# Softmax reciprocals on their way through DRAM: 16 bytes a partition instead of single elements, in an adaLN block on one core

## The chip, the cores and the metric

One Trainium2 chip, one of its cores. A core has five engines that run side by side, each its own list of instructions in order: TensorE (PE) for matmuls, VectorE (DVE), ScalarE (ACT), GpSimd (POOL) and SyncE (SP). Here SP issues nearly all DMA transfers, and 16 DMA engines carry them out. Engines wait for each other, and for transfers, by semaphores. The metric is the device time of one execution in microseconds (us), as the median of several runs.

## The reference

One transformer block, sequence 2048, width 576, in float32. Attention has 32 query heads on 16 cached key/value heads of width 128, and looks at the last 512 cached keys.

```python
h = layernorm(x) * (1 + ca) + sa
q = (h @ wq) per head                       # 32 heads of 128
scores = q @ k[last 512 keys]^T * 128**-0.5
p = softmax(scores); o = p @ v              # two query heads share a k and a v
x = x + ga * (o @ wo)
h = layernorm(x) * (1 + cb) + sb
x = x + gb * ((sigmoid(h @ w_gate) * (h @ w_up)) @ w_down)
```

sa, ca, ga, sb, cb, gb are six rows of silu(c) @ w_mod. The change touches the softmax's division alone: o is the unnormalised product with v, times one over the row's sum.

## The kernel before

The kernel runs in stages: the projection of q (to about 460 us), attention (about 460 to 2380 us), the product with wo, and the gated feed-forward part. All float32 operands are split in a high and a low part, and products are made of three matmuls each.

**Attention** is a list of 128 blocks (`NBLK`). A block is one head and 512 query rows, in four tiles of 128 rows (`TPB` = 4). A loop (lines 1296 to 1325) takes one step n for each tile, so a block is four steps. The step works on several blocks at once, in a software pipeline: `scores` three steps ahead (three matmuls of 128x512 into the tile st, and on VectorE the negated row maximum neg), `expo` two steps ahead (ScalarE writes pp, the exponentials, and their row sum into one column of sum), `transp` (four TensorE transposes of pp into pt; ScalarE and VectorE copy them out, high and low, into ptt), and `pv` five steps behind (three matmuls a step into ot, the output with its 128 features on the partitions and 512 query rows along the free dimension). Tasks that are due at a step's start or end stand in tables (`at_n`, `at_late`).

**The division.** After the fourth tile of block b, VectorE takes the reciprocal of sum (128 partitions x 4 tiles, line 814) into rs. In rs a query row is a partition and a column; in ot a query row is a place in the free dimension, the same for every partition. So rs has to be turned and copied to all partitions, and that goes by way of DRAM: `put_rs` (line 874) stores rs in a scratch tensor rscr of 2 KB, and `get_rs` (line 877) reads it back, broadcast to all 128 partitions, into rb (128x512). Four scratch tensors are used in turn. `ov_out` (line 860) then multiplies ot by rb on VectorE into ov. For the last two blocks the turn is made with TensorE (`spread_rs`, `spread_mm`), and rscr isn't used; so there are 126 stores and 126 reads.

In steps: block b's sums are complete in step 4b+1. `put_rs` is due at the end of step 4b+2, `get_rs` at the end of 4b+5, and `ov_out` at the end of 4b+10.

**SP's list** holds all of this in the order of the program: put_rs, get_rs, a load of q for a later block (qr from qscr), every second block a store of ov (to oscr), every eighth block loads of k and v (kv), and the background work: weights of wo, w_gate, w_up and w_down are loaded into rooms (x, xr), combined and split by GpSimd and ScalarE, and stored in DRAM for the later stages (wosc, dsc, wsc), 5 to 28 transfers a job, a job about every two blocks. The read in get_rs needs the store in put_rs to have landed, so SP stops at get_rs until then, with everything behind it. VectorE in its turn stops at ov_out's multiplication until rb has landed, and behind that stand neg and ptt, which TensorE and ScalarE need.

In the store of before, rscr is laid out tile by tile (4 x 128), and a partition's four values go to four places that are 512 bytes apart, so that each value is a piece of its own, of 4 bytes.

Nearly every instruction is recorded on line 36, a helper, so that the profile is read by the names of the tiles.

Of the kernel before, what the change touches and what calls it, by code (L numbers as in the profile page):

```python
# [9 lines left out]
F32 = mybir.dt.float32  # L10
# [6 lines left out]
P = 128  # L17
BLK = 512
TPB = BLK // P
# [25 lines left out]
def adaln_block_kernel(ctx: ExitStack, tc: tile.TileContext, x, k_cache, v_cache, wq, wo, w_gate, w_up, w_down,  # L45
                       c, w_mod, out):
    early = [True]
    nc = Ordered(tc, early, tc.nc)
# [15 lines left out]
    NBLK = NB * H  # L64
# [5 lines left out]
    dram = ctx.enter_context(tc.tile_pool(name="dram", bufs=1, space=bass.MemoryType.DRAM))  # L70
# [32 lines left out]
    def keep_order(i):  # L103
        if held[0]:
            tc.keep_in_program_order(i)
# [638 lines left out]
    SUM, RS, RB, PP, PT, OT, OP_ = {}, {}, {}, {}, {}, {}, {}  # L744
# [10 lines left out]
    def blk_of(b):  # L755
        return seq[b]
# [46 lines left out]
    def expo(n):  # L803
        b, i = divmod(n, TPB)
        half, hd, blk = blk_of(b)
        if n % 3 == 2 and n < N - 9:
            PP[n] = pools["wp2"].tile([P, W], F32, tag="pp", name="pp", bufs=1)
        else:
            PP[n] = at.tile([P, W], F32, tag="pp", name="pp", bufs=2)
        keep_order(nc.scalar.activation(PP[n], ST.pop(n), AF.Exp, bias=NEG[b][:, i : i + 1],  # L810
                                        accum_out=SUM[b][:, i : i + 1]))
        if i == TPB - 1:
            RS[b] = at.tile([P, TPB], F32, tag="rs", name="rs", bufs=3)
            nc.vector.reciprocal(RS[b], SUM[b])
            if b < NBLK - 2:
                at_late(n - 1, put_rs, b)
                at_late(n + 2, get_rs, b)
            else:
                spread_rs(b)
                at_late(n + (0 if b == NBLK - 2 else 1), spread_mm, b)  # L820
            if last_of[half * H + hd] == b:
                m = n + (5 if b == NBLK - 1 else 9)
                if not summed(half, hd):
                    at_late(m, put_o, half, hd)
                elif hd % 2:
                    at_late(n + 8, sum_o, hd)
                    at_n(n + 15, put_sx, hd, (0, 1))
                    at_n(n + 15, put_o, half, hd - 1)
                    at_n(n + 19, put_o, half, hd)
                    at_late(n + 19, sum_last, hd)  # L830
                    at_n(n + 24, put_sx, hd, (2,))
# [14 lines left out]
    def pv(b, k):  # L846
        half, hd, blk = blk_of(b)
        if k == 0:
            OP_[b] = bank("ot", 2, pools["psa"])
        v = VS[hd // REP]  # L850
        t = PT[b]
        mm_seq(OP_[b], three(v[:, 0, k, :], v[:, 1, k, :], t[:, 0, k, :], t[:, 1, k, :]),
               first=k == 0, last=k == KT - 1)
        if k == KT - 1:
            if b < NBLK - 2:
                at_late(TPB * b + 10, ov_out, b)
            else:
                ov_out(b)

    def ov_out(b):  # L860
        half, hd, blk = blk_of(b)
        unit = (half, hd)
        if unit not in OT:
            own = b // 2 % 4 == 3 and b < NBLK - 12
            OT[unit] = pools["wp2" if own else "ov"].tile([P, TPB, 2, P], F32, tag="ov", name="ov", bufs=1 if own else 3)
        by_tile = RB.pop(b).rearrange("p (i q) -> p i q", i=TPB)
        nc.vector.tensor_mul(OT[unit][:, :, blk % 2, :], OP_[b].rearrange("p (i q) -> p i q", i=TPB), by_tile)
        del OP_[b]

    rscr = [dram.tile([TPB, P], F32, tag=f"rscr{i}", name=f"rscr{i}") for i in range(4)]  # L870
    oscr = [[dram.tile([P, TPB, 4, 4, P], F32, tag=f"oscr{h}_{q}", name=f"oscr{h}_{q}") for q in range(H // 8)]
            for h in range(2)]

    def put_rs(b):
        keep_order(nc.sync.dma_start(rscr[b % 4].rearrange("t p -> p t"), RS[b]))

    def get_rs(b):
        RB[b] = pools["at2"].tile([P, BLK], F32, tag="rb", name="rb", bufs=2)
        keep_order(nc.sync.dma_start(RB[b], rscr[b % 4].rearrange("t p -> (t p)").partition_broadcast(P)))

    def spread_rs(b):
        DG[b] = at.tile([P, TPB, P], F32, tag="qt", name="dg", bufs=2)
# [414 lines left out]
    for n in range(NLO, N + TPB + 5):  # L1297
# [12 lines left out]
        b, i = divmod(n - 5, TPB)  # L1310
# [349 lines left out]
    for v in range(VISITS):  # L1660
        q, pair, t = VISIT[v]
        banks = {}
        for s, (plane, combo, tag, row, col) in enumerate(STAGES):
# [5 lines left out]
            p = banks[tag]  # L1669
# [192 lines left out]
```

## Time and profile before

| | |
|---|---|
| time, median of 3 runs | 3988.19 us (3988.03 to 3992.52) |
| the profiled execution | 3987.48 us, its span from the first to the last instruction 3985.7 us |
| PE / DVE / ACT / POOL busy | 81% / 55% / 46% / 46% of the span |
| granted TensorE clock, mean of the span | 0.90 |
| attention, window 470 to 2340 us | PE busy 1163.82 of 1870 us, granted clock 0.80 |
| DMA over the span | 637.25 MB in 558469 packets, 159 GB/s |

A row of a group in the profile names engine, operation, the tile written and the tiles read, the shape, and how often; behind the bar stand the busy time in us, the mean of one in ns, and the idle time of the engine just before such instructions with what ended it. A row of waits names the engine and what it wrote, what it waited for, the sum in us, how often, and the longest. A row of windows has the stretch, then for PE, its weight loads, DVE, ACT and POOL the busy time with the number of instructions, and last the granted clock, the busy share of the 16 DMA engines and the GB/s that they moved. "SPq" is SP issuing: a DMA's row on SP shows its issue and not its transfer. The chain of waits is followed back from the last instruction; a piece in it that begins with DMA reaches from the transfer's issue to what it released.

### The profile page before, as it was taken

To read this page: it belongs to the slowest core of one execution; us is meant where nothing else is said; L and a number is where in the kernel's file an instruction comes from. 1 tells how busy PE (TensorE), PEld (TensorE's weight loads), DVE (VectorE), ACT (ScalarE), POOL (GpSimd) and SP (SyncE) were. 2 spreads that over 40 slices of the span, in tenths; PEclk is the share of its full clock that TensorE was granted. 3 is DMA by queue.
4 is the path that set the end of the run, shared out by engine and by line. 5 is a ranking of instruction groups with operands and counts; after the bars stand their busy time and mean duration, and the time that the engine had idled before them with its cause. 6 is when DMAs were issued, how large, how long until landed. Compare 5 with 4: busy or idle time off the path is not lost.

```text
span 3985.7 us, 49960 instructions
## 1 busy us (share of the span) xinstructions
PE 3209.4 (81%) x16375; PEld 2696.1 (68%) x16375; DVE 2200.4 (55%) x3908; ACT 1819.5 (46%) x3663; POOL 1845.6 (46%) x1685
## 2 busy tenths in 40 slices
PE   8989865665666666665566669999999999999999
PEld 6767654444554444444445559998888888888888
DVE  6775443343443444333434448887666667666667
ACT  5554443444444444433334334465444445444443
POOL 4646333444555455321221115523676555565555
PEclk9999987787888788777788879999999999999999
DMA  5748787876898677786867964576556555655554
GB/s 171 244 137 240 194 133 131 153 167 134 157 157 169 147 170 148 157 135 128 135 127 93 129 153 179 216 256 205 167 149 171 163 141 160 190 142 144 142 143 120
DMA packets 558469, 637.25 MB, mean 160 GB/s; under 512 B 104576, under 2 KB 478208, under 8 KB 549504
## 3 DMA queue, kind: packets, MB, share of 16 engines
q1 hardware_dynamic: 557072, 633.53, 67.0%
q8 instruction: 129, 2.11, 0.3%
q14 instruction: 132, 1.08, 0.1%
q10 hardware_dynamic: 1136, 0.53, 0.0%
HBM read 426.64 MB, written 207.25 MB: 159 GB/s over the span
## 4 chain that ended last, share of the span: by engine, by line
PE 46%; DMA 37%; SPq 6%; DVE 4%; issue 3%; ACT 2%; POOL 2%; ACTq 0%; POOLq 0%; DVEq 0%
PE a L36 19%; DMA rscr<-rs 19%; PE w L36 10%; PE c L36 10%; SPq L36 6%; DMA rb<-rscr 5%; PE b L36 5%; DMA qr<-qscr 3%; DMA wosc<-xr 1%; DMA dsc<-xr 1%; DMA dsc<-x 1%; DMA oscr<-ov 1%; PE ot L36 1%; DMA qscr<-qo 1%; DMA wsc<-xr 1%
## 5 line engine op out<-in xcount | busy, mean ns | idle before, releaser
L36 PE MATMUL ot<-ptt,vs 128*128 128x512 f32 x1536 | 534.7, 463 | 534.4 <-DVE ptt L36 534.1
L36 PEld LDWEIGHTS ot<-ptt,vs 128*128 128x128 f32 x1536 | 336.2, 226 | 659.4 <-DVE ptt L36 584.5
L36 ACT ACTIVATE pp<-st,neg 128x512 f32<-128x512 f32 x512 | 351.1, 686 | 662.8 <-DVE neg L36 658.6
L36 PE MATMUL a<-hc,sw 128*128 128x512 f32 x2016 | 584.9, 396 | 1.4 <-DVE v L36 1.3
L36 PE MATMUL st<-kt,qt 128*128 128x512 f32 x1536 | 558.3, 477 | 12.8 <-DVE kt L36 12.7
L36 POOL TENSOR_TENSOR qt<-qr,qt 128x512 fp32r<-128x512 f32 x128 | 163.9, 1280 | 837.4 <-ACT qt L36 810.6
L36 DVE TENSOR_TENSOR x<-w,x 128x288 f32<-128x288 f32 x964 | 418.6, 451 | 238.5 <-PE w L36 235.0
L36 DVE TENSOR_TENSOR ptt<-pt,ptt 128x512 fp32r<-128x512 f32 x512 | 352.5, 689 | 271.0 <-ACT ptt L36 270.7
L36 DVE TENSOR_TENSOR ov<-ot,rb 128x512 f32<-128x512 f32 x128 | 88.5, 691 | 742.9 <-DMA rb<-rscr 723.9
L36 PE MATMUL pt<-ident,pp 128*128 128x128 f32 x2048 | 361.3, 306 | 99.0 <-DVE ptt L36 99.0
L36 PEld LDWEIGHTS pt<-ident,pp 128*128 128x128 f32 x2048 | 296.8, 161 | 199.0 <-DVE ptt L36 116.6
L36 PEld LDWEIGHTS a<-hc,sw 128*128 128x128 f32 x2016 | 356.4, 188 | 41.8 <-DVE v L36 2.8
L36 ACT ACTIVATE ptt<-pt 128x512 fp32r<-128x512 f32 x512 | 304.9, 596 | 160.1 <-PE pt L36 159.0
L36 DVE TENSOR_REDUCE neg<-st 128x1 f32<-128x512 f32 x512 | 348.9, 681 | 7.2 <-PE st L36 7.1
L36 ACT ACTIVATE sw<-sr 128x384 fp32r<-128x384 f32 x504 | 257.5, 519 | 190.9 <-issue 90.1
L36 PEld LDWEIGHTS w<-wh,hl 128*128 128x128 f32 x1776 | 297.1, 188 | 52.7 <-DVE x L36 3.1
L36 PE MATMUL w<-wh,hl 128*128 128x288 f32 x1776 | 328.2, 296 | 0.8 <-DVE x L36 0.7
L36 PEld LDWEIGHTS st<-kt,qt 128*128 128x128 f32 x1536 | 296.1, 222 | 45.0 <-DVE kt L36 13.4
L36 POOL TENSOR_TENSOR sw<-sr,sw 128x256 fp32r<-128x256 f32 x245 | 184.7, 754 | 281.9 <-ACT sw L36 279.0
L36 PE MATMUL c<-hc,sw 128*128 128x512 f32 x1008 | 304.0, 395 | 0.0
L36 DVE TENSOR_TENSOR sw<-sr,sw 128x256 fp32r<-128x256 f32 x259 | 188.6, 729 | 141.6 <-ACT sw L36 140.3
L36 POOL TENSOR_TENSOR hl<-vs,hl 128x512 fp32r<-128x512 f32 x139 | 192.0, 1382 | 107.5 <-ACT hl L36 106.2
(299 smaller groups left out, 5933.7 us busy)
## 6 DMA issues: line engine op xcount, KB each, us to landing
sr<-wsc SPq DMA_DIRECT2D x504, 192.0 KB
wh<-dsc SPq DMA_DIRECT2D x144, 288.0 KB
qscr<-qo SPq DMA_DIRECT2D x128, 256.0 KB
qr<-qscr SPq DMA_DIRECT2D x128, 256.0 KB
vr<-oscr SPq DMA_DIRECT2D x32, 1024.0 KB
rb<-rscr SPq DMA_DIRECT2D x126, 256.0 KB
oscr<-ov SPq DMA_DIRECT2D x63, 512.0 KB
wsc<-x SPq DMA_DIRECT2D x26, 896.0 KB
```

The lines of the kernel that those rows point to most:

```text
L36: i = got(*args, **kw)
```

## The change

Three places, none of which adds, removes or moves an instruction on any engine. rscr is laid out partition by partition (128 x 4). The store writes a partition's four values as one piece of 16 bytes. The broadcast reads the same 2 KB in a row as before, so that rb holds the values in another order: the four tiles' values of one partition side by side. `ov_out` reads rb with a view that puts them in the order of ot, which makes neighbouring elements of VectorE's second input lie 16 bytes apart (not in the last two blocks, whose rb comes from TensorE in the old order).

```diff
-        by_tile = RB.pop(b).rearrange("p (i q) -> p i q", i=TPB)
+        by_tile = RB.pop(b).rearrange("p (q i) -> p i q" if b < NBLK - 2 else "p (i q) -> p i q", i=TPB)
         nc.vector.tensor_mul(OT[unit][:, :, blk % 2, :], OP_[b].rearrange("p (i q) -> p i q", i=TPB), by_tile)
...
-    rscr = [dram.tile([TPB, P], F32, tag=f"rscr{i}", name=f"rscr{i}") for i in range(4)]
+    rscr = [dram.tile([P, TPB], F32, tag=f"rscr{i}", name=f"rscr{i}") for i in range(4)]
...
     def put_rs(b):
-        keep_order(nc.sync.dma_start(rscr[b % 4].rearrange("t p -> p t"), RS[b]))
+        keep_order(nc.sync.dma_start(rscr[b % 4], RS[b]))
...
-        keep_order(nc.sync.dma_start(RB[b], rscr[b % 4].rearrange("t p -> (t p)").partition_broadcast(P)))
+        keep_order(nc.sync.dma_start(RB[b], rscr[b % 4].rearrange("p t -> (p t)").partition_broadcast(P)))
```

## The prediction

> **What bounds the kernel now.** I read the page's chain first, for the lines that hold the end; then the waits of attention by engine; then, for one block, what SP and the DMA engines did. The page's chain, shares of the span by engine and by line:
>
> ```profile
> PE 46%; DMA 37%; SPq 6%; DVE 4%; issue 3%; ACT 2%; POOL 2%; ACTq 0%; POOLq 0%; DVEq 0%
> PE a L36 19%; DMA rscr<-rs 19%; PE w L36 10%; PE c L36 10%; SPq L36 6%; DMA rb<-rscr 5%; PE b L36 5%; DMA qr<-qscr 3%; DMA wosc<-xr 1%; DMA dsc<-xr 1%; DMA dsc<-x 1%; DMA oscr<-ov 1%; PE ot L36 1%; DMA qscr<-qo 1%; DMA wsc<-xr 1%
> ```
>
> 19% of 3985.7 us, 757 us, hang on the store of rscr: 126 transfers of 2 KB. In the middle of attention (470 to 2340 us) the waits of SP, of TensorE and of VectorE begin with these rows:
>
> ```profile
> SPq L36 <- DMA rscr<-rs: 948.7, 111, 16.4
> SPq L36 <- DMA wosc<-xr: 18.4, 11, 3.8
> ...
> PE ot L36 <- DVE ptt L36: 524.3, 102, 18.0
> PE pt L36 <- DVE ptt L36: 85.8, 32, 8.8
> PE st L36 <- DMA kv<-in_A_k_cache_dram: 77.3, 15, 12.6
> ...
> DVE ov L36 <- DMA rb<-rscr: 714.1, 115, 19.1
> ```
>
> SP spends half of the window waiting for that store. VectorE waits 714.1 us for rb, which SP couldn't read earlier; TensorE waits for ptt, which stands behind that multiplication on VectorE. So one ring of waits sets the pace: SP's list, with the store's landing in it. The next wait of SP is fifty times smaller. What the engines do meanwhile, in windows of the projection of q and of attention:
>
> ```profile
> 100.00:200.00 100.00, 93.53 (x397) 73.53 (x396) 75.87 (x137) 53.34 (x88) 64.84 (x68) 0.98 0.80 245
> 470.00:2340.00 1870.00, 1163.82 (x5095) 908.42 (x5094) 747.15 (x1276) 791.41 (x1777) 687.77 (x605) 0.80 0.77 140
> ```
>
> In attention no engine is full: TensorE is busy 62% of the time at a granted clock of 0.80, ScalarE 42%, VectorE 40%. A DMA share of 0.77 looks like a full queue, but it comes with 140 GB/s, where the projection got 245 GB/s with a share of 0.80: the transfers are held up, not numerous. SP's rows for the store and the read give the pace (issue min/median/max in ns, first and last start):
>
> ```profile
> L36 SPq DMA_DIRECT2D rscr<-rs x126: 370/384/2809, 469.0 to 2338.6; - x126
> L36 SPq DMA_DIRECT2D rb<-rscr x126: 319/326/1903, 487.5 to 2351.7; - x126
> ```
>
> From the first read to the last there are 1864.2 us and 125 blocks, **14.91 us a block**. Of these SP waits 948.7 / 125 = **7.59 us** for the store; the other **7.32 us** are its issues and its small waits.
>
> Why does a store of 2 KB take so long? One block shows it undisturbed: SP's list, then the DMA engines in two windows.
>
> ```profile
> 2169.09 0.38 SPq L36 DMA_DIRECT2D rscr<-rs  x1
> 2177.16 0.34 SPq L36 DMA_DIRECT2D rb<-rscr  x1
> ...
> 2170.00:2172.00 2.00, 1.57 (x4) 1.18 (x5) 1.80 (x4) 2.00 (x5) 0.27 (x1) 0.50 0.16 6
> 2172.00:2177.00 5.00, 5.00 (x21) 4.11 (x20) 2.34 (x5) 2.68 (x8) 1.00 (x1) 0.68 0.00 0
> ```
>
> The read follows the store directly, 2177.16 - 2169.09 = **8.07 us** after it. For the last 5 us the DMA engines have no packet to move (share 0.00), and the store has not yet landed: its writes are on the way into DRAM. The chain has ordinary stores of 256 KB, in the projection, beside them three stores of rscr and one of ov from attention (start, us):
>
> ```profile
> 65.50 2.39 DMA qscr<-qo
> 138.31 6.79 DMA qscr<-qo
> ...
> 596.76 14.32 DMA rscr<-rs
> 626.71 9.72 DMA rscr<-rs
> 640.97 16.04 DMA oscr<-ov
> 658.16 13.93 DMA rscr<-rs
> ```
>
> 128 times as many bytes in 128 pieces land in 2.39 us when nothing is in the way, so the 8.07 us are not a price of bytes. What differs is 512 pieces of 4 bytes.
>
> **The change part by part.** *The store: 512 pieces of 4 bytes become 128 of 16.* The quiet store costs 8.07 us; an ordinary one with 128 pieces 2.39 us. If the excess goes by pieces, one piece costs (8.07 - 2.39) / 512 = 11.1 ns, and 128 of them 1.42 us: the new store lands in 2.39 + 1.42 = 3.81 us, and **4.26 us** a block go. The ends: 2.39 us if small pieces then cost nothing extra (5.68 us go), 8.07 us if the excess hangs on something that stays, such as the 2 KB of DRAM that are touched (nothing goes). I take pieces, since the count is the one thing that sets this store apart from qscr's.
>
> The Trainium skill (DMA: Bandwidth & Descriptors, Specifications) says that below 512 bytes a transfer makes a read and a write of each piece's surroundings; 16 bytes are as much below that as 4, so by the page alone the new pieces stay slow ones. By it the cost of one piece stays and their number is a quarter, which is my term; if what is read and rewritten is the same 512 bytes each time and these queue, it is the second end. No row here has pieces between 4 and 512 bytes in a store.
>
> *What the slow writes do to others.* The quiet store is the shortest: 9.72 to 14.32 us stand above, 1.65 to 6.25 us more. Ordinary stores vary as well, by 6.79 - 2.39 = 4.40 us, so most of that excess is other traffic; but the store of ov that was issued behind a store of rscr needed 16.04 us. Issues show it too: SP's rows for one load in attention (ns, min/median/max):
>
> ```profile
> L36 SPq DMA_DIRECT2D x<-in_A_wo_dram x44: 448/1130/7379, 618.6 to 1054.9; - x44
> ```
>
> Its issue takes 0.448 us where nothing holds it, 1.130 us at the median and up to 7.4 us. Some of this goes with the slow writes. Bounds: 0 us a block, and the 3.33 us that are left of SP's wait (7.59 - 4.26). I take **1.3 us**, a fifth of the largest excess, nearer to zero because the big transfers stay.
>
> *The sum on SP's ring.* 7.59 - 4.26 - 1.3 = 2.03 us of wait are left, with the 7.32 us beside it 9.35 us a block. Is something else late then? TensorE's rows where it ran without a gap, at a granted clock of 1.0, start of the transposes of two steps:
>
> ```profile
> 901.61 0.60 PE L36 MATMUL pt<-ident,pp 128*128 128x128 f32 x4
> ...
> 903.44 0.60 PE L36 MATMUL pt<-ident,pp 128*128 128x128 f32 x4
> ```
>
> A step is 1.83 us, a block 7.32 us. ScalarE is busy 791.41 / 125.4 = 6.31 us a block (1870 us are 125.4 blocks), VectorE 5.96, GpSimd 5.48. For DMA, the volume of the window:
>
> ```profile
> DMA packets 286618, 262.45 MB, mean 140 GB/s; under 512 B 79920, under 2 KB 244654, under 8 KB 285760
> ```
>
> 262.45 MB are 2.09 MB a block; at the projection's 245 GB/s these take 8.5 us. All of these are below 9.35 us, though the DMA's not by much, so the ring's sum stands: 14.91 - 9.35 = 5.56 us a block, x 126 = **701 us**.
>
> *The read of rb* moves the same bytes in the same pieces: no change. *No instruction moves*, so no queue is passed in another order.
>
> *The multiplication in ov_out* reads rb with 16 bytes between elements. Its row now (ns), and the slowest row of this shape on any engine, both with all inputs in a row:
>
> ```profile
> L36 DVE TENSOR_TENSOR ov<-ot,rb x128: 680/692/693, 492.1 to 2375.2; 128x512 f32<-128x512 f32 x128
> ...
> L36 POOL TENSOR_TENSOR qt<-qr,qt 128x512 fp32r<-128x512 f32 x128 | 163.9, 1280 | 837.4 <-ACT qt L36 810.6
> ```
>
> No row shows a stride of 16 bytes on VectorE. Bounds: no change (0.69 us), and twice, 1.38 us, about the 1.28 us of the other row; nothing here could make it faster. I take no change in the sum: at 9.35 us a block VectorE's 5.96 us leave 3.4 us, which hide either end. Without that cover it costs up to 0.69 x 126 = 87 us.
>
> Total: the profiled execution's 3987.48 us (span and 1.8 us around it) less 701 is 3286 us; its distance to the median, 0.7 us, is nothing here. **I predict 3285 us.**
>
> **The rivals.** *A: the store's landing improves, but the traffic ahead of it holds the ring.* Then the 1.3 us aren't got, and more of the 4.26 us is lost behind the megabyte-sized stores (wosc, dsc) in the same queue. For it: landings of 9.72 to 14.32 us against 8.07, and 8.5 us a block for the bytes alone. Against it: in attention the bytes flow at 140 GB/s only. It gives 10.65 us a block with all of the 4.26 us (537 us, 3450), 12.8 us with half (268 us, 3719): 3450 to 3720.
>
> *B: the stride turns it round.* VectorE pays for each element's own 16 bytes, and the store gains nothing. VectorE stands on the ring today (714.1 us of waiting for rb, and TensorE behind it), so the dearer multiplication follows each wait in full: 87 us, 4075 us. It decides as soon as the store gains less a block than the multiplication loses, 0.69 us at most. For it: no row shows the stride as free. Against it: a gain under 0.69 us from a quarter of the pieces.
>
> The Trainium skill (SBUF — State Buffer, Door 1: The DMA port swizzle) speaks for this one: it says that an engine that goes to another 16-byte line with each access pays a penalty, which is just this stride for float32. No run so far shows it.
>
> *C: the change does not do what it is for.* The landing stays at about 8 us because the excess hangs on the 2 KB, or on the way back of the acknowledgment, and the stride is free: 3988 us, within 8. Against it: 2.39 us for a store 128 times as large.
>
> *D: TensorE becomes the bound*, the DMA follows at more than 245 GB/s: from 8.5 us down to 7.32 us a block, 808 to 956 us, 3031 to 3180 us.
>
> **How the numbers follow.** Forecast (3180 to 3450) 0.62; A 0.22; B 0.05; C 0.05; D 0.06. A measurement of this kernel can tell about 0.2%, 8 us, from no change. Faster: 0.62 + 0.22 + 0.06 = 0.90. Same is C, 0.05; slower is B, 0.05. The range leaves out B and C, the lower half of D and the upper third of A, 0.2 together: 3130 to 3640 us.
>
> **What would show it.** Right: in the profile after, the quiet store of rscr is followed by its read within 3 to 5 us, not 8; SP's wait for rscr<-rs in attention falls from 948.7 us to 100 to 400; VectorE's wait for rb falls with it; attention ends near 1680 us in place of 2380; the granted clock there rises from 0.80, since TensorE's idle stretches get short; the DMA moves over 200 GB/s. The multiplication into ov shows the price of the stride at once, 0.69 or more. Wrong: SP still waits some 7 us a block (C or B), or its wait is gone and another transfer's stands in its place, or the background stores' (A). If SP waits little and the time still doesn't fall, my reading that SP sets the pace is wrong.

## The result, and the profile after

| | before | changed |
|---|---|---|
| time, median of 4 runs each (for the kernel before, one more than above) | 3990.22 us | 3222.57 us (3220.72 to 3232.8) |
| ratio, with its 95% interval | 1 | **0.8081 [0.8063, 0.8099]** |
| profiled execution | 3987.48 us | 3232.8 us, span 3231.0 us |
| granted TensorE clock, mean of the span | 0.90 | 0.974 |

768 us are gone, 19%; 703 were forecast (3988 - 3285). The time has gone from attention alone, whose last read of rb begins at 1595.4 us in place of 2351.7 (rows of SP, start of the first and the last):

```profile
L36 SPq DMA_DIRECT2D rscr<-rs x126: 319/383/2269, 467.4 to 1590.9; - x126
L36 SPq DMA_DIRECT2D rb<-rscr x126: 319/330/1305, 480.4 to 1595.4; - x126
```

That is (1595.4 - 480.4) / 125 = **8.92 us a block**, where it was 14.91. The chain, by engine and by line, and the waits in attention (470 to 1585 us) of SP, TensorE and VectorE:

```profile
PE 64%; DMA 13%; DVE 7%; ACT 5%; SPq 5%; issue 4%; POOL 3%; ACTq 0%; POOLq 0%; DVEq 0%
PE a L36 24%; PE c L36 12%; PE w L36 12%; PE b L36 6%; DMA rb<-rscr 5%; SPq L36 5%; PE ot L36 4%; PE st L36 4%; DMA rscr<-rs 4%; PE pt L36 2%; DVE neg L36 1%; ACT pp L36 1%; DVE sw L36 1%; ACT ptt L36 1%; DVE ptt L36 1%
```

```profile
SPq L36 <- DMA rscr<-rs: 343.0, 90, 9.2
SPq L36 <- POOL qt L36: 24.1, 20, 4.2
...
PE ot L36 <- DVE ptt L36: 112.7, 39, 12.5
...
DVE ptt L36 <- ACT ptt L36: 165.3, 351, 3.0
DVE ov L36 <- DMA rb<-rscr: 142.1, 42, 13.2
```

The store has gone from 19% of the chain to 4%. SP waits 343.0 us for it in place of 948.7, VectorE 142.1 us for rb in place of 714.1, TensorE 112.7 us for ptt in place of 524.3. The store is still SP's longest wait, but it no longer holds every block. The window of attention, and the quietest store with its read on SP:

```profile
470.00:1585.00 1115.00, 970.91 (x4994) 786.11 (x4993) 772.12 (x1252) 773.31 (x1747) 688.31 (x604) 0.94 0.80 235
```

```profile
1304.38 0.41 SPq L36 DMA_DIRECT2D rscr<-rs  x1
1306.83 0.34 SPq L36 DMA_DIRECT2D rb<-rscr  x1
```

TensorE is busy 87% of the stage at a granted clock of 0.94 (62% and 0.80 before). The DMA engines have nearly the same share as before, 0.80 against 0.77, and move 235 GB/s in place of 140 with it. For about the same 262 MB each DMA engine is busy 0.80 x 1115 = 892 us now and was busy 0.77 x 1870 = 1440 us before. The store itself has 126 x 384 = 48384 packets fewer, but the packets of other transfers are held for a shorter time too: the 59700 packets of 512 bytes between the first and the last read of rb took 55 ns in the mean before and 30 ns now, the longest 6.98 us and 2.42 us. The quiet store is read after 2.45 us, not 8.07 us. And VectorE does pay for the stride (ns, min/median/max):

```profile
L36 DVE TENSOR_TENSOR ov<-ot,rb x128: 691/1074/1109, 484.9 to 1620.2; 128x512 f32<-128x512 f32 x128
```

### The profile page after: what moved, and what is told of

Its sections match the earlier page's. It is cut to its first block, busy times and chain, and to the rows that moved or that the text cites. A ratio compares the mean times of both kernels' runs of the same rounds, so it can differ in the third digit from the quotient of the medians.

```text
span 3231.0 us, 49960 instructions
## 1 busy us (share of the span) xinstructions
PE 3030.8 (94%) x16375; PEld 2585.7 (80%) x16375; DVE 2237.5 (69%) x3908; ACT 1814.1 (56%) x3663; POOL 1847.3 (57%) x1685
## 4 chain that ended last, share of the span: by engine, by line
PE 64%; DMA 13%; DVE 7%; ACT 5%; SPq 5%; issue 4%; POOL 3%; ACTq 0%; POOLq 0%; DVEq 0%
PE a L36 24%; PE c L36 12%; PE w L36 12%; PE b L36 6%; DMA rb<-rscr 5%; SPq L36 5%; PE ot L36 4%; PE st L36 4%; DMA rscr<-rs 4%; PE pt L36 2%; DVE neg L36 1%; ACT pp L36 1%; DVE sw L36 1%; ACT ptt L36 1%; DVE ptt L36 1%
## 5 line engine op out<-in xcount | busy, mean ns | idle before, releaser
L36 PE MATMUL ot<-ptt,vs 128*128 128x512 f32 x1536 | 462.9, 411 | 113.2 <-DVE ptt L36 112.9
L36 PE MATMUL st<-kt,qt 128*128 128x512 f32 x1536 | 502.3, 436 | 3.7 <-POOL qt L36 3.7
L36 PEld LDWEIGHTS ot<-ptt,vs 128*128 128x128 f32 x1536 | 296.6, 196 | 203.3 <-DVE ptt L36 136.0
L36 PEld LDWEIGHTS pt<-ident,pp 128*128 128x128 f32 x2048 | 265.2, 145 | 82.7 <-DVE ptt L36 11.0
L36 PE MATMUL pt<-ident,pp 128*128 128x128 f32 x2048 | 319.7, 280 | 8.1 <-DVE ptt L36 8.1
L36 PEld LDWEIGHTS st<-kt,qt 128*128 128x128 f32 x1536 | 261.6, 197 | 31.6 <-POOL qt L36 4.9
L36 DVE TENSOR_TENSOR ov<-ot,rb 128x512 f32<-128x512 f32 x128 | 136.6, 1067 | 151.8 <-DMA rb<-rscr 142.1
```

The lines of the kernel that those rows point to most:

```text
L36: i = got(*args, **kw)
```

## The experiments

The kernels ran on several chips, on which the kernel before took 3944 to 3990 us. So each is given as a ratio to the kernel before on its own chip, with the 95% interval. The "quiet" store is the shortest time in the profile from the issue of a store of rscr to the issue of the read that follows. How well ratios of different chips agree wasn't measured, so a difference of about 0.01 between them is weak: nostride, stride, eight_byte and spaced_64 ran on one chip, one_engine, spaced_16, beside and turned on a second, cluster, beside_spaced and hop on a third.

| kernel | pieces of the store | in each 64 bytes | quiet, us | ratio |
|---|---|---|---|---|
| before | 512 of 4 bytes | 16 | 8.07 | 1 |
| one_engine | 512 of 4 bytes | 16 | 8.19 | 1.0344 [1.0312, 1.0376] |
| eight_byte | 256 of 8 bytes | 8 | 3.67 | 0.8619 [0.8590, 0.8647] |
| changed | 128 of 16 bytes | 4 | 2.45 | 0.8081 [0.8063, 0.8099] |
| spaced_16 | 512 of 4 bytes | 4 | 2.75 | 0.8202 [0.8185, 0.8219] |
| cluster | 512 of 4 bytes | 4 | 3.26 | 0.8317 [0.8302, 0.8333] |
| spaced_64 | 512 of 4 bytes | 1 | 2.06 | 0.8039 [0.8007, 0.8071] |
| turned | 4 of 512 bytes | - | 1.21 | 0.7976 [0.7963, 0.7989] |

The first theory was the prediction's: the store's landing closes SP's ring, its excess goes by the number of pieces, and the stride is covered.

**The stride alone, in both kernels.** In the changed kernel the view of before, and in the kernel before the changed view:

```diff
-        by_tile = RB.pop(b).rearrange("p (q i) -> p i q" if b < NBLK - 2 else "p (i q) -> p i q", i=TPB)
+        by_tile = RB.pop(b).rearrange("p (i q) -> p i q", i=TPB)
```

> The changed kernel, but the multiplication into ov reads rb in a row, as before, so each value meets the wrong row of the softmax (the division's result is left wrong; all work is there). It takes the stride alone out of the changed kernel, where that multiplication takes 1067 ns against 692 before: 0.375 us a block, 126 times, 47 us of VectorE. Theory 1 (VectorE's time is covered, the pace of attention is set by TensorE and by what is left of the store's wait): 3222 us, within 8. Rival (VectorE stands on the chain with every block): 47 us less, 3175 us.

> The kernel before, with its store of 4-byte pieces, but the multiplication into ov reads rb with 16 bytes between elements (values in the wrong order; all work is there). Theory 1 (VectorE waits for rb in nearly each block, so what the multiplication takes longer follows the wait): up to 47 us over 3990, 4037 us, with ov at about 1067 ns. Rival (the ring on SP has room for it, since the store's landing and not VectorE closes the ring): 3990 us, within 8.

Measured: nostride 0.8118 [0.8091, 0.8144], stride 0.9992 [0.9973, 1.0011]. The multiplication's rows, first without the stride in the changed kernel, then with it in the kernel before:

```profile
L36 DVE TENSOR_TENSOR ov<-ot,rb x128: 680/682/694, 487.0 to 1606.6; 128x512 f32<-128x512 f32 x128
```

```profile
L36 DVE TENSOR_TENSOR ov<-ot,rb x128: 692/1051/1116, 490.7 to 2343.6; 128x512 f32<-128x512 f32 x128
```

The stride costs VectorE about 0.37 us a time in either kernel, and the time of neither (in full, 47 us would be 0.012 of the ratio). Taking it out gains nothing (0.8118 against 0.8081, not lower); putting it in costs nothing, although VectorE waits for rb in nearly every block there: this fits a ring that SP closes, in which 0.37 us on VectorE have room beside SP's next wait.

**Half way.** rscr as [2, P, 2], pieces of 8 bytes (against the changed kernel; the read and the multiplication's view follow the layout and are left out):

```diff
-    rscr = [dram.tile([P, TPB], F32, tag=f"rscr{i}", name=f"rscr{i}") for i in range(4)]
+    rscr = [dram.tile([2, P, 2], F32, tag=f"rscr{i}", name=f"rscr{i}") for i in range(4)]
...
-        keep_order(nc.sync.dma_start(rscr[b % 4], RS[b]))
+        keep_order(nc.sync.dma_start(rscr[b % 4].rearrange("h p j -> p h j"), RS[b].rearrange("p (h j) -> p h j", h=2)))
```

> The changed kernel with pieces of 8 bytes: rscr as two halves of 128 x 2, so 256 pieces, and neighbouring elements of rb 8 bytes apart for the multiplication. Quiet store to read: 8.07 us with 512 pieces of 4 bytes, 2.45 us with 128 of 16. Theory 1 (the excess goes by the number of pieces, in a straight line between the two): 2.45 + 5.62 x 128 / 384 = 4.3 us, and the time about a third of the way back, 3222 + 768 / 3 = 3480 us, less if the landing still fits in the three steps between store and read. Rival (a piece is slow when it is under 16 bytes, whatever the number): the landing stays above 6 us and the time above 3700 us. Second rival (there is a number of pieces under which nothing queues): 2.5 us and 3222 us.

Measured: 0.8619, 3412 us. The quiet store, and VectorE's multiplication, whose second input has a stride of 8 bytes here:

```profile
1427.37 0.41 SPq L36 DMA_DIRECT2D rscr<-rs  x1
1431.04 0.34 SPq L36 DMA_DIRECT2D rb<-rscr  x1
```

```profile
L36 DVE TENSOR_TENSOR ov<-ot,rb x128: 680/692/693, 485.4 to 1794.2; 128x512 f32<-128x512 f32 x128
```

Of the gain 28% is given back, where a third was expected (3480 us, a ratio of 0.872), and the quiet store takes 3.67 us (4.3 expected). Neither rival's times are met: a piece isn't as slow as before just for being under 16 bytes. A smooth dependence fits the number of pieces, but number and closeness still change together.

**The number kept, the distance changed.** The kernel before, with the same 512 pieces 64 bytes apart (what fills rscr's first 2 KB once at the start is left out):

```diff
-    rscr = [dram.tile([TPB, P], F32, tag=f"rscr{i}", name=f"rscr{i}") for i in range(4)]
+    rscr = [dram.tile([TPB, P, 16], F32, tag=f"rscr{i}", name=f"rscr{i}") for i in range(4)]
...
-        keep_order(nc.sync.dma_start(rscr[b % 4].rearrange("t p -> p t"), RS[b]))
+        keep_order(nc.sync.dma_start(rscr[b % 4][:, :, 0].rearrange("t p -> p t"), RS[b]))
...
-        keep_order(nc.sync.dma_start(RB[b], rscr[b % 4].rearrange("t p -> (t p)").partition_broadcast(P)))
+        keep_order(nc.sync.dma_start(RB[b], rscr[b % 4].rearrange("t p s -> (t p s)")[:BLK].partition_broadcast(P)))
```

> The kernel before with the same 512 pieces of 4 bytes, but 64 bytes apart in DRAM (rscr is 16 times as large, four tiles of 32 KB, their first 2 KB filled once at the start); the read takes the first 2 KB as it did, so the division's values are mostly wrong and all other work is there. Theory 1 (the number of pieces makes the store slow): quiet store to read stays at 8 us, 3990 us within 40. Rival (pieces that lie side by side in DRAM get in each other's way): the landing falls to 2.4 to 4 us and the time to 3175 to 3300 us, a little under the changed kernel since the multiplication has no stride.

Measured: 0.8039. The quiet store, still of 512 pieces of 4 bytes, and SP's wait for it (470 to 1532 us):

```profile
1452.35 0.40 SPq L36 DMA_DIRECT2D rscr<-rs  x1
1454.41 0.34 SPq L36 DMA_DIRECT2D rb<-rscr  x1
```

```profile
SPq L36 <- DMA rscr<-rs: 266.6, 84, 8.2
```

**The number of pieces is out as the cause.** 512 pieces of 4 bytes are as quick as 128 of 2 KB (2.06 us; 2.39 in the projection's chain) when they lie apart. Second theory: what costs is how many pieces lie in the same 64 bytes of DRAM.

**Side by side, but from one place in the list.** In the changed kernel, a gap behind each value of rs in SBUF makes 512 pieces of 4 bytes again, in the order of DRAM:

```diff
-            RS[b] = at.tile([P, TPB], F32, tag="rs", name="rs", bufs=3)
+            RS[b] = at.tile([P, TPB, 2], F32, tag="rs", name="rs", bufs=3)[:, :, 0]
```

> The changed kernel, layout and stride as there, but rs has a gap behind each value in SBUF, so that the store is 512 pieces of 4 bytes again, in the order in which they lie in DRAM: 16 pieces side by side in each 64 bytes, as before, but a partition's four and its neighbours' come one after the other. All values are right. The run with pieces 64 bytes apart has ruled out the number. Theory 2 (what costs is how many pieces lie in the same 64 bytes: 16 before, 8 with pieces of 8 bytes, 4 with the change, 1 when spaced): quiet store to read 8 us, the time that of before, ratio 0.97 to 1.01. Rival (what costs is that pieces of the same 64 bytes are written from different places in the list of pieces, so by several DMA engines at once: four before, fewer here): quiet store to read 2.5 to 4 us, ratio 0.81 to 0.85.

Measured: 1.0344, slower than before. The quiet store, and SP's wait (470 to 2441 us):

```profile
1923.47 0.56 SPq L36 DMA_DIRECT2D rscr<-rs  x1
1931.66 0.34 SPq L36 DMA_DIRECT2D rb<-rscr  x1
```

```profile
SPq L36 <- DMA rscr<-rs: 1037.7, 113, 16.0
```

The second theory holds, with more than expected (0.97 to 1.01); its rival asked for a quiet store of 2.5 to 4 us, and it takes 8.19. It is also the changed kernel's layout and stride with nothing but the size of the pieces put back: the layout by itself brings nothing.

**Four in 64 bytes, in two ways.** spaced_16 is spaced_64 with `[TPB, P, 4]`. cluster is the changed kernel with a partition's four 4-byte pieces side by side and the next partition's 64 bytes further on:

```diff
-            RS[b] = at.tile([P, TPB], F32, tag="rs", name="rs", bufs=3)
+            RS[b] = at.tile([P, TPB, 2], F32, tag="rs", name="rs", bufs=3)[:, :, 0]
...
-    rscr = [dram.tile([P, TPB], F32, tag=f"rscr{i}", name=f"rscr{i}") for i in range(4)]
+    rscr = [dram.tile([P, 4 * TPB], F32, tag=f"rscr{i}", name=f"rscr{i}") for i in range(4)]
...
-        keep_order(nc.sync.dma_start(rscr[b % 4], RS[b]))
+        keep_order(nc.sync.dma_start(rscr[b % 4][:, :TPB], RS[b]))
...
```

> The kernel before with its 512 pieces of 4 bytes, 16 bytes apart in DRAM (rscr is 8 KB; its first 2 KB are filled once, the read takes these, so most values of the division are wrong; all other work is there): four pieces in each 64 bytes, as in the changed kernel with its 16-byte pieces. Theory 2 (pieces in the same 64 bytes, whatever their size and number): as the changed kernel with no stride, ratio 0.81, quiet store to read 2.5 us. Rival (small pieces are dear side by side, and bytes that are left out between them don't help until they are 64 bytes apart, or the size of 4 bytes counts too): between before and that, ratio 0.85 to 0.95, quiet 4 to 6 us.

> The changed kernel's layout spread out: 512 pieces of 4 bytes, a partition's four side by side in 16 bytes, the next partition's 64 bytes further on; so four pieces in each 64 bytes, as with pieces 16 bytes apart (ratio 0.820), but these four touch each other and 48 bytes stay empty. rscr is 8 KB, its first 2 KB are filled once and read, so most values of the division are wrong; all other work is there. Theory 2 (pieces in the same 64 bytes, wherever they lie in them): ratio 0.81 to 0.83, quiet store to read 2.5 to 3.5 us. Rival (pieces must touch, or lie in the same 16 or 32 bytes, to be slow): ratio above 0.90, quiet above 5 us.

Measured: 0.8202 and 0.8317. The quiet store of the first and of the second:

```profile
1498.66 0.41 SPq L36 DMA_DIRECT2D rscr<-rs  x1
1501.41 0.34 SPq L36 DMA_DIRECT2D rb<-rscr  x1
```

```profile
1558.53 0.40 SPq L36 DMA_DIRECT2D rscr<-rs  x1
1561.79 0.34 SPq L36 DMA_DIRECT2D rb<-rscr  x1
```

Both are near the changed kernel (0.8081, without its stride 0.8118), as the second theory has it, and neither is at the rivals' 0.85 or 0.90. cluster is a hair over the 0.83 expected and 0.0115 above spaced_16, on another chip. Its pieces touch, but they are also written in the order of their addresses, which went with 0.0344 in one_engine; so whether the place within the 64 bytes counts isn't shown. That the unit is 64 bytes, and not some other stretch of that order, isn't shown: 16, 8, 4 and 1 pieces in 64 bytes were tried, and these are different densities over any longer stretch too.

**The old store beside the new one.** Is it the landing in SP's ring that cost, or what the slow writes do to others? The changed kernel, with the old store as an extra that nobody reads:

```diff
+    dscr = [dram.tile([TPB, P], F32, tag=f"dscr{i}", name=f"dscr{i}") for i in range(4)]
...
         keep_order(nc.sync.dma_start(rscr[b % 4], RS[b]))
+        keep_order(nc.sync.dma_start(dscr[b % 4].rearrange("t p -> p t"), RS[b]))
```

> The changed kernel with one more store a block, right behind put_rs: the same rs in the old way, 512 pieces of 4 bytes side by side, into a scratch tensor of its own that nobody reads (126 transfers more, all values right). It parts the two effects of the old store: its landing in SP's wait, which is not there, and what its writes do to other transfers, which is. Theory 1 (the landing in the ring is nearly all; other transfers get 1.3 us a block at most): 0.4 us of issue and up to 1.3 us a block, 126 times, 0 to 215 us more than the changed kernel, ratio 0.81 to 0.86. Rival (the slow writes hold up whatever stands behind them, the read of rb first): more than half of the gain goes, ratio above 0.90.

Measured: 0.9626 [0.9611, 0.9641], far above what the theory allowed. SP over one block, then a piece of the chain, the waits of SP and the window of attention (470 to 2146 us):

```profile
1505.30 0.38 SPq L36 DMA_DIRECT2D qr<-qscr  x1
1505.73 0.42 SPq L36 DMA_DIRECT2D rscr<-rs  x1
1506.20 0.42 SPq L36 DMA_DIRECT2D dscr<-rs  x1
...
1517.07 1.44 SPq L36 DMA_DIRECT2D rb<-rscr  x1
```

```profile
1505.30 11.51 DMA qr<-qscr
```

```profile
SPq L36 <- DMA rscr<-rs: 524.9, 90, 13.1
SPq L36 <- DMA dscr<-rs: 95.9, 38, 6.3
```

```profile
470.00:2146.00 1676.00, 1107.00 (x5032) 871.13 (x5031) 781.13 (x1260) 781.45 (x1756) 686.95 (x605) 0.82 0.80 156
```

The new store's read comes 11.3 us after it, though it stands ahead of the old store in the list, and the load of q ahead of both needs 11.51 us (the old store of the block before was issued 11.4 us ahead of that load). The DMA engines are back at a low rate, 156 GB/s, with a share of 0.80. So it looks as if the extra store held up loads and stores that have nothing to do with it. Whether the place of its pieces does that, or the transfer as such, is told by the control, which has the same extra transfer with its pieces 64 bytes apart (`dscr` as [TPB, P, 16]):

> The control to the run with the old store beside: the changed kernel with the same additional store of 512 pieces of 4 bytes behind put_rs, which nobody reads, but its pieces 64 bytes apart (all values right). Theory 3 (what the pieces side by side do in DRAM holds up the other transfers, and this made most of the old time): the extra store is then only 0.5 us of SP's issue a block, ratio 0.81 to 0.83. Rival (126 more transfers of 512 pieces on SP's list and on the DMA engines are themselves what cost 0.15): ratio 0.93 to 0.96, as with the old store beside.

Measured: 0.8253 [0.8236, 0.8271]; SP's wait in its attention (470 to 1628 us) is under the changed kernel's, and the rate is nearly the changed kernel's:

```profile
SPq L36 <- DMA rscr<-rs: 295.1, 86, 7.2
```

```profile
470.00:1628.00 1158.00, 977.86 (x5006) 788.87 (x5006) 774.46 (x1255) 775.13 (x1751) 688.64 (x605) 0.93 0.83 227
```

ScalarE's wait for the loads of q, first with the old store beside (470 to 2146 us), then in the control:

```profile
ACT qt L36 <- DMA qr<-qscr: 81.6, 31, 6.7
```

```profile
ACT qt L36 <- DMA qr<-qscr: 0.2, 1, 0.2
```

So pieces that lie side by side hold up transfers that have nothing to do with them. The extra transfer itself costs 0.8253 - 0.8081 = 0.017, the closeness of its pieces 0.9626 - 0.8253 = 0.137, which is 72% of the gain (0.192) and 4.3 us a block. Two things limit what this says. SP isn't quite free of the old store: 95.9 us of its waits are put down to that store's landing. And nearly all of the price can come by way of the ring again: the read of rb follows the new store after 10.70 us at the median with the old store beside, and after 6.62 us in the control, 4.1 us of the 4.3.

**A longer ring without slow writes.** The changed kernel, with a copy of the 2 KB within DRAM between store and read, which SP waits for too:

```diff
+    hscr = [dram.tile([P, TPB], F32, tag=f"hscr{i}", name=f"hscr{i}") for i in range(4)]
...
+        keep_order(nc.sync.dma_start(hscr[b % 4].rearrange("(a p) t -> a (p t)", a=TPB),
+                                     rscr[b % 4].rearrange("(a p) t -> a (p t)", a=TPB)))
-        keep_order(nc.sync.dma_start(RB[b], rscr[b % 4].rearrange("p t -> (p t)").partition_broadcast(P)))
+        keep_order(nc.sync.dma_start(RB[b], hscr[b % 4].rearrange("p t -> (p t)").partition_broadcast(P)))
```

> The changed kernel with one more landing in SP's ring and no slow writes: get_rs first copies the 2 KB from rscr to a second scratch tensor in DRAM (16 pieces of 128 bytes), and the broadcast reads that, so SP waits twice a block (all values right). The second landing costs about as much as the quiet store, 2.45 us and 0.4 us of issue: 2.9 us a block. Theory 1 (each us of landing in the ring is a us of the block): 2.9 x 126 = 365 us more, ratio 0.89 to 0.91. Theory 3 (the old time was mostly that other transfers were held up; a landing that holds up nobody is partly covered by the three steps between store and read): under half of it, ratio 0.81 to 0.855.

Measured: 0.8786 [0.8769, 0.8802]. SP's waits (470 to 1829 us):

```profile
SPq L36 <- DMA hscr<-rscr: 311.0, 124, 5.7
SPq L36 <- DMA rscr<-rs: 278.2, 85, 9.2
```

0.0705 more than the changed kernel is 279 us on this chip, 2.2 us a block, for a second landing that SP waits 2.5 us for (311.0 / 124) and 0.4 us of issue. That lies between the two expectations, nearer to the first: a microsecond of landing in the ring is here about three quarters of a microsecond of the block. So the old store's own landing and what it does to other transfers both have a price; they aren't two sums to be added, since a transfer that is held up can be the one that SP waits for.

**A version that is faster than both.** rs turned on TensorE first, then stored as 4 pieces of 512 bytes:

```diff
+                at_late(n - 1, turn_rs, b)
...
+    def turn_rs(b):
+        p = ps_st()[:TPB, :P]
+        nc.tensor.transpose(p, RS[b], ident)
+        RT[b] = pools["wp2"].tile([TPB, P], F32, tag="rt", name="rt", bufs=2)
+        keep_order(nc.scalar.activation(RT[b], p, AF.Copy))
...
-        keep_order(nc.sync.dma_start(rscr[b % 4].rearrange("t p -> p t"), RS[b]))
+        keep_order(nc.sync.dma_start(rscr[b % 4], RT.pop(b)))
```

> The kernel before, but rs is turned on TensorE first (a transpose of 128 x 4 into a bank of st, copied by ScalarE to 4 partitions x 128), and the store is 4 pieces of 512 bytes; the layout of rscr, the read and the multiplication are those of before, without a stride. All values are right. Theory 2 (few large pieces don't share anything): the store lands as in the run with pieces 64 bytes apart, for some 0.3 us of TensorE and 0.3 us of ScalarE a block: ratio 0.80 to 0.81, under the changed kernel's 0.808 if the two additions are covered. Rival (the extra transpose stands in TensorE's list before the next scores and waits for the reciprocal there): 0.5 us a block and more, ratio 0.82 or above.

Measured: 0.7976 [0.7963, 0.7989], 3144 us against 3944 on its chip: under the changed kernel's interval, and under the 0.80 expected. The quiet store, SP's wait and the window of attention (470 to 1493 us):

```profile
608.37 0.27 SPq L36 DMA_DIRECT2D rscr<-rt  x1
609.58 0.33 SPq L36 DMA_DIRECT2D rb<-rscr  x1
```

```profile
SPq L36 <- DMA rscr<-rt: 198.6, 75, 7.8
```

```profile
470.00:1493.00 1023.00, 945.82 (x5098) 772.87 (x5097) 725.42 (x1249) 793.49 (x1863) 687.92 (x604) 0.97 0.80 255
```

The read follows after 1.21 us, the DMA engines move 255 GB/s, and TensorE is busy 92% of the stage. The lead over the changed kernel, 0.0105, is one between chips, but the block is shorter too, 8.21 us against 8.92. The transposes and copies that it adds are nearly covered: SP waits 36.8 us in all for the copies.

## Why the prediction was right, and where it was not

**The bound was read rightly.** SP's ring with the store's landing in it set the pace. The wait for the store fell and took VectorE's and TensorE's waits along; the hop shows the ring from the other side. The stage ended near 1620 us (1680 was forecast), the granted clock rose to 0.94, and the rate to 235 GB/s, between the 200 and 245 GB/s that were named.

**The step on the pieces failed: "If the excess goes by pieces, one piece costs 11.1 ns", and "I take pieces, since the count is the one thing that sets this store apart".** The count was not the one thing: 512 pieces 64 bytes apart land in 2.06 us. Closeness in DRAM was the other, and no row of the profile before parts them. The change cut both by four, and so the wrong one gave a term of about the right size; that was luck. The quiet store fell to 2.45 us and not to 3.81, under the 3 to 5 us that were named as a sign, so the term was 5.62 us where 4.26 were taken; the lower end of its bounds, 2.39 us, was nearly reached.

**The step on other transfers, 1.3 us, was too large as a term of the sum.** The block lost 5.99 us, so 5.99 - 5.62 = 0.37 are left for it. Of the 14.91 us a block, SP's issues and small waits, held fixed at 7.32, fell to 6.18. Its wait of 7.59 us would have come to 1.97 by the quiet store alone and came to 343.0 / 125 = 2.74. The reading "most of that excess is other traffic" isn't contradicted: the read followed the store after 12.18 us at the median before and after 6.31 us now, which is 4.1 and 3.9 us above the quiet store. The load's issue, read as a sign, kept its median (1.130 us before, 1.212 now) and lost only its longest, 7.379 us before (ns, min/median/max):

```profile
L36 SPq DMA_DIRECT2D x<-in_A_wo_dram x44: 430/1212/2656, 555.9 to 823.1; - x44
```

That the slow writes hold others up is true, and the old store beside the new one costs 0.137 by it. But in the ring a long landing and a transfer that is held up can be one and the same wait, and the prediction added them as two terms.

**The sum came out near because the errors were on both sides**, which is luck again: the store's term was 1.36 us too small, the other 0.93 us too large. Forecast were 5.56 us a block, measured 5.99.

**The stride's cost was between its bounds and covered**, as taken: 1.07 us, against 0.69 and 1.38. The Trainium skill's warning (SBUF — State Buffer, Door 1: The DMA port swizzle) is borne out on VectorE: 16 bytes between elements cost 0.38 us, 8 bytes, with two elements in each 16, nothing (692 ns). Rival B needed the store to gain less than that.

**The rivals.** A had a queue of large transfers keep the ring at 10.65 us a block or more; the block takes 8.92. The bytes don't set that pace, since the turned version moves 255 GB/s. C fell with the landing. D, TensorE as the bound from 8.5 down to 7.32 us a block, is what the turned version comes near, with 8.21 us a block.

The rule of the Trainium skill that was weighed (DMA: Bandwidth & Descriptors, Specifications: below 512 bytes a read and a write of the surroundings) gives no price here by itself: pieces of 16 bytes (2.45 us), and even of 4 when they lie apart (2.06 us), land about as fast as pieces of 2 KB (2.39 us). No run shows a read or a rewrite, and why close pieces are slow stays open.

## What to carry to other kernels

A small transfer that an in-order queue waits for can cost most of its landing in every turn of the loop, about three quarters here; look in the profile for a wait in which the DMA engines have nothing to move. Don't scatter a store over single elements that lie side by side in DRAM: here such writes delayed other transfers as well, which showed as a high DMA share at a low rate (0.77 at 140 GB/s). Where TensorE has room, turn small data there first and write few, long pieces, which was the fastest version here.

## What the runs showed of the hardware that had not been expected

- 512 writes of 4 bytes into the same 2 KB land in 8.07 us with the DMA engines idle for the last 5 us; the same 512 writes, each 64 bytes from the next, land in 2.06 us. With 16, 8 and 4 pieces in each 64 bytes it is 8.07 to 8.19, 3.67 and 2.45 to 3.26 us.
- While such writes are under way, others wait: the packets of 512 bytes in attention took 55 ns in the mean before and 30 with the change, 53 with the old store beside the new one and 32 in its control; a load of 256 KB took 11.51 us with the old store beside the new one. Whether they wait in DRAM, or in the DMA engines behind writes that are not acknowledged, stays open.
- Writing them in the order of their addresses doesn't help: that kernel was 3.4% slower than with the scattered order, with the stride that costs no time by itself (0.9992).
- VectorE's product of 128x512 in float32 with an input in PSUM takes 692 ns with its other input's elements 4 or 8 bytes apart in SBUF, and 1074 ns with 16 bytes.
